# Other durations for small matmuls and for GpSimd's DMA issues in the planner of a fused attention and two-layer kernel

## The chip, the cores and the metric

One core of a Trainium2 chip runs the whole program. The metric is the device time of one execution in microseconds (us), the median of several runs. The core has five engines, each with its own instruction queue worked off in order: TensorE (PE), VectorE (DVE), ScalarE (ACT), GpSimd (POOL) and SyncE (SP). A DMA is issued from one of these queues, here from SP's and POOL's, and the queue stands still while its next instruction waits for a semaphore.

## The reference

```python
gamma = 1.0 - 2.0 ** (-5.0 - np.arange(H))              # B=4, H=8, S=768, D=64
for t in range(S):
    state = gamma * state + einsum('bhd,bhe->bhde', k[:, :, t], v[:, :, t])
    y[:, :, t] = scale * einsum('bhd,bhde->bhe', q[:, :, t], state)
x = y as 3072 tokens x 512
h = x @ w_in;   x = (h * sigmoid(1.702 h)) @ w_out      # 512 -> 2048 -> 512
h = x @ w2_in;  g = P(h) / Q(h);  out = g @ w2_out      # rational function, 512 -> 2048 -> 512
```

Everything is fp32. The kernel keeps that accuracy by splitting each operand of the two layers into a high and a low part and running three products of them.

## The kernel before

The program has three stretches. Up to some 138 us a first block of work is emitted in an order written out by hand (the steps 0 to 13 of layer 1 with the attention chunks they need). From about 138 to 608 us runs the rest of layer 1, interleaved with attention and with the preparation of layer 2's weights; this is the stretch that a list scheduler orders. From 608 us to the end layer 2 runs by a planner of its own.

In the middle stretch the code calls the engines as usual, but while `nc.on` is set each call is only recorded, as an operation of the class `Deck`. `Deck.cost` (L281) gives it a duration from its engine and its shape. `Deck.plan` (L314) then plays the program: it always takes the engine that can go on earliest and of its ready operations the one that was recorded first; a DMA's landing is estimated from its size and its run length. `Deck.flush` (L370) emits the operations in the planned order, so that each engine's queue follows the plan. All instructions of this stretch therefore carry L375 in the profile; L390 is work that was not recorded. Calls inside `with nc.group(extra)` stay together as one operation whose duration is their sum plus `extra`. The order within each engine is fixed by this plan; at run time only semaphores decide when an instruction starts. Tiles of one pool tag share slots, and the plan decides which slot a tile gets and which earlier reader it must wait for.

Attention runs in 24 chunks of 128 tokens, six for each batch. Chunks 8 to 23 belong to the recorded stretch. The names of a chunk c, which the later sections use with the chunk's number behind them:

- q and k are loaded "turned" by 16 small DMAs each (`load_turned`), q's on SyncE's queue, k's on GpSimd's, into slots of the tag "raw". These slots appear in the profile under the name of whoever opened them (`turnq_slot`, `turnk_slot`, `rawk_slot`, `rawv_slot`): the turned q of chunk 18, for example, lies in `turnk_slot`.
- `att_turn` multiplies the turned q with a table on VectorE (`<-turnq_slot,qtab`) and transposes both (`STREAM_TRANSPOSE qT`, `kT`). A transpose ends the use of its raw slot.
- `y_unit(c)` (L1533) issues a group of small 64x64 matmuls on TensorE: the sums of the state and the outputs of the chunk's first half. It needs the masked scores sm(c) (two VectorE products, `sm_slot<-pS_slot,cs`). VectorE then makes the two states st (`st_slot<-pS_slot,st_slot`). The unit ends with the load of turned q and k of chunk c + 2.
- `z_unit(c)` (L1544) issues the outputs of the second half, which need the states, and the scores of chunk c + 1, which need qT and kT of c + 1. The masks sm(c + 1) follow on VectorE. `out` and `lows` copies turn the outputs into high and low parts (`xh`, `xl`).

y16, z16 and so on below are the groups of small matmuls of these units. Between two such groups TensorE runs the large matmuls (128x512 output) of layer 1: `hp_slot<-xh_slot,wi` for the hidden layer, `o_slot<-gh_slot,wo` for its output, with `gl` and `gh` the parts of the activation, made on VectorE and ScalarE.

Beside that, `conv2` prepares layer 2's weights: a 512 KB load on SyncE into a staging tile (`os`, `sumb`, `a`), a first pass on ScalarE into `u`, a handful of passes on VectorE (`TENSOR_SCALAR`, `SCALAR_TENSOR_TENSOR`, `TENSOR_TENSOR` on `os`, `sumb`, `a`, `u`), and a store to `wc` or `wo` in DRAM on GpSimd. A staging tile is loaded anew once its stores have been read out.

Of the kernel before, what the change touches and what calls it, by code (L numbers as in the profile page):

```python
# [233 lines left out]
class Deck:  # L234
# [46 lines left out]
    def cost(self, engine, method, out, views):  # L281
        if method == "dma_start":
            size = 1
            for v in views[:1]:
                size = v.at.size * (P // ROWS if v.home.space != "dram" else 1)
            return (0.4 if engine == "sync" else 0.7), size * 4
        n = int(np.prod(out.shape[1:])) if isinstance(out, View) else 64
        if engine == "tensor":
            return (0.2267 if n >= 512 else 0.0178 * n / 64), None
        if engine == "scalar":  # L290
            return 0.19 + n * 0.00083, None
        if method == "tensor_scalar":
            return 0.155 + n * 0.00052, None
        return 0.155 + n * 0.00104, None
# [515 lines left out]
def tile_kernel(ctx: ExitStack, tc: tile.TileContext, q, k, v, w1i, w1o, w2i, w2o, pa, pb, cst, out):  # L810
    nc = Deck(tc)
# [280 lines left out]
    def load_raw(c, nm, pool=None, tag="raw", at=None):  # L1092
        b, cc = divmod(c, NCH)
        src = {"q": q, "k": k, "v": v}[nm][b, :, cc * P : (cc + 1) * P, :]
        t = at
        if t is None:
            t = (pool or raws).tile([P, H, D], F32, tag=tag, name=f"raw{nm}{c}")
        if nm == "v" or (c < 4 and nm == "q"):
            nc.sync.dma_start(out=t, in_=src.rearrange("h t d -> t h d"), run=256)
        else:  # L1100
            pairs = t.rearrange("t (p n) d -> t n p d", n=2)
            for n in range(2):
                nc.sync.dma_start(out=pairs[:, n], in_=src[NP * n : NP * n + NP].rearrange("p t d -> t p d"), run=256)
        RAW[c, nm] = t
# [29 lines left out]
    def scale_v(c, eng):  # L1134
        v_ = RAW[c, "v"]
        f = tab["k"][:, c % NCH, :]
        if eng is nc.scalar:
            for x in range(H):
                h = v_[:, NP * (x % 2) + x // 2]
                nc.scalar.activation(out=h, in_=h, func=ACTF.Copy, scale=f[:, x : x + 1])  # L1140
        else:
            o = v_.rearrange("a (n p) d -> a n p d", n=2)
            g = f.rearrange("a (p n) -> a n p", n=2)
            eng.tensor_tensor(out=o, in0=o, in1=g.unsqueeze(3).to_broadcast([P, 2, NP, D]), op=ALU.mult)
# [5 lines left out]
    def ps(tag, nm):  # L1150
        if tag in "ah":
            return (ps_a if tag == "a" else ps_h).tile([P, NP, P], F32, tag=tag, name=nm)
        return ps_o.tile([P, NP, P], F32, tag=tag, name=nm)
# [18 lines left out]
    def load_turned(c, nm, eng):  # L1172

        b, cc = divmod(c, NCH)
        src = {"q": q, "k": k}[nm][b, :, cc * P : (cc + 1) * P, :]
        t = raws.tile([P, NP, P], F32, tag="raw", name=f"turn{nm}{c}")
        for g in range(4):
            for p in range(NP):
                eng.dma_start(
                    out=t[32 * g : 32 * g + 32, p, :].rearrange("j (b i) -> j b i", i=32),  # L1180
                    in_=src[NP * (g // 2) + p, :, 32 * (g % 2) : 32 * (g % 2) + 32].rearrange("(b j) i -> j b i", j=32),
                    run=128,
                )
        RAW[c, nm + "T"] = t
# [15 lines left out]
    def scores(c, pss, col, flip):  # L1200

        qT, kT = QK[c, "q"], QK.pop((c, "k"))
        for p in range(NP):
            for n in range(2):
                for x in range(2):
                    r, w = HALF[n], HALF[x]
                    nc.tensor.matmul(
                        pss[n ^ flip][w, col + 64 * p : col + 64 * p + 64], kT[r, p, w], qT[r, p, w],
                        start=(p == 0), stop=True, skip_group_check=True,
                    )  # L1210

    def masks(c, pss, col, flip, alt=None):
        sm = at_tile(c, "sm", alt).rearrange("a (n x) t -> a n (x t)", n=2).rearrange("a n (p t) -> a n p t", t=D)
        for n in range(2):
            nc.vector.tensor_tensor(
                out=sm[:, n], in0=pss[n ^ flip][:, col : col + 4 * D].rearrange("a (p t) -> a p t", t=D), in1=mask, op=ALU.mult
            )
        SM[c] = sm
# [47 lines left out]
    def state_sums(c, pss, begun):  # L1266

        kr, vr = RAW.pop((c, "k")), RAW[c, "v"]
        for p in range(NP):
            for x in state_halves(c):  # L1270
                for n in range(2):
                    w = HALF[x]
                    nc.tensor.matmul(
                        pss[x][HALF[n], 4 * D + 64 * p : 4 * D + 64 * p + 64], kr[w, 2 * p + n, :], vr[w, NP * n + p, :],
                        start=(x, n) not in begun, stop=True, skip_group_check=True,
                    )
                    begun.add((x, n))

    def states_of(c, pss):

        state = ST.get(c)
        for x in state_halves(c):
            pk = pss[x][:, 4 * D :].rearrange("a (p e) -> a p e", e=D)
            t = (at1, sp)[x].tile([P, NP, D], F32, tag=("mid", "st")[x], name=f"st{x}_{c}")
            if state is None:
                nc.vector.tensor_copy(out=t, in_=pk)
            else:
                nc.vector.tensor_tensor(out=t, in0=pk, in1=state, op=ALU.add)
            state = t
            ST[(c, "mid") if x == 0 else c + 1] = t  # L1290

    def att_S(c, tg, alt=None, sums=True):
        pss = [ps(tg[n], f"pS{n}_{c}").rearrange("a x t -> a (x t)") for n in range(2)]
        with nc.group(0.25):
            scores(c, pss, 0, 0)
        if sums:
            state_sums(c, pss, {(x, n) for x in range(2) for n in range(2)})
        masks(c, pss, 0, 0, alt)
        if sums:
            states_of(c, pss)  # L1300
# [222 lines left out]
    def out_home(c):  # L1523
        bi, cc = divmod(c, 4)
        if bi < NB:
            if cc == 0:
                x_tiles(bi)
            return (*X[1, bi], cc * P)
        t = at.tile([P, H, D], F32, tag="raw", name=f"so{c}")
        t = SO[c] = t.rearrange("a (n k h) d -> a n k (h d)", n=2, k=2)  # L1530
        return [t[:, 0], t[:, 1]], None, 0

    def y_unit(c):  # L1533
        with nc.group(0.25):
            att_Y0(c, ("a", "a"), *out_home(c), True, PIECES)
        PIECES[c][0]()
        states_of(c, PY[c])
        if c + 1 < NT // P:
            scale_v(c + 1, nc.vector)
        if c + 2 < NT // P:  # L1540
            load_turned(c + 2, "q", nc.sync)
            load_turned(c + 2, "k", nc.gpsimd)

    def z_unit(c):  # L1544
        py = PY.pop(c)
        _, second, outs, lows = PIECES.pop(c)
        with nc.group(0.25):
            second()
            if c + 1 < NT // P:
                scores(c + 1, py, 4 * D, 1)  # L1550
        outs()
        if c + 1 < NT // P:
            masks(c + 1, py, 4 * D, 1)
        lows()
        if c + 2 < NT // P:
            load_raw(c + 2, "k")
            load_raw(c + 2, "v")

    def s_unit(c):
        att_S(c, ("a", "a"), None, False)  # L1560
        scale_v(c, nc.vector)
        att_turn(c + 1)
# [14 lines left out]
    for c in range(FLAT, NT // P):  # L1577
        n = c - FLAT
        todo[Y_AT[n]].append(lambda c=c: y_unit(c))
        todo[Z_AT[n]].append(lambda c=c: z_unit(c))  # L1580
        if c + 2 < NT // P:
            todo[TURN_AT[n]].append(lambda c=c: att_turn(c + 2))
# [18 lines left out]
    with tc.manual_schedule(engines={E.SP}):  # L1601
# [198 lines left out]
        with tc.manual_schedule(engines={E.PE, E.DVE, E.Activation, E.Pool}):  # L1800
# [109 lines left out]
            for i in range(FIRST_STEPS, NS - 2):  # L1910
# [12 lines left out]
                layer, bi, fc, t0, n = steps[i]  # L1923
# [193 lines left out]
```

## Time and profile before

| | before |
|---|---|
| median of 3 runs | 1101.42 us (1100.48 to 1102.96) |
| profiled execution, own time | 1104.64 us |
| its span | 1102.8 us |
| granted TensorE clock, mean | 0.999 of full speed |
| TensorE busy | 1087.5 us, 99% of the span |
| VectorE busy | 872.2 us, 79% |
| ScalarE busy | 698.5 us, 63% |
| GpSimd busy | 208.0 us, 19% |

The profile is of one execution, whose own time lies 3.22 us above the median; of its time 1.84 us lie outside the span. A timeline row gives the start of an instruction (or of several alike in a row) from the span's start, its length, engine, line, operation with output and inputs, count, and in brackets the idle time just before it with what ended it. The instructions of one engine overlap a little, so the distance of two starts is a better measure of a cost than the length.

### The profile page before, as it was taken

To read this page: it belongs to the slowest core of one execution; us is meant where nothing else is said; L and a number is where in the kernel's file an instruction comes from. 1 tells how busy PE (TensorE), PEld (TensorE's weight loads), DVE (VectorE), ACT (ScalarE), POOL (GpSimd) and SP (SyncE) were. 2 spreads that over 40 slices of the span, in tenths; PEclk is the share of its full clock that TensorE was granted. 3 is DMA by queue.
4 is the path that set the end of the run, shared out by engine and by line. 5 is a ranking of instruction groups with operands and counts; after the bars stand their busy time and mean duration, and the time that the engine had idled before them with its cause. 6 is when DMAs were issued, how large, how long until landed. Compare 5 with 4: busy or idle time off the path is not lost.

```text
span 1102.8 us, 19408 instructions
## 1 busy us (share of the span) xinstructions
PE 1087.5 (99%) x7169; PEld 883.0 (80%) x7169; DVE 872.2 (79%) x1262; ACT 698.5 (63%) x1105; POOL 208.0 (19%) x368
## 2 busy tenths in 40 slices
PE   8999999999999999999999999999999999999998
PEld 6678878888877778888888888888888888888886
DVE  6898556356745679789995799998988897899895
ACT  5898422233323346667763788787787886787882
POOL 0003346545675601133102000000000000000000
PEclk9999999999999999999999999999999999999999
DMA  9964336546776775798878775832454913454011
GB/s 229 318 174 131 77 113 165 141 103 153 194 195 158 219 233 200 236 364 311 290 254 329 267 247 202 315 153 86 126 153 130 333 51 96 124 162 117 19 39 39
DMA packets 192703, 199.76 MB, mean 181 GB/s; under 512 B 108512, under 2 KB 140768, under 8 KB 192608
## 3 DMA queue, kind: packets, MB, share of 16 engines
q1 hardware_dynamic: 172960, 154.45, 46.7%
q0 software_dynamic: 19648, 44.06, 11.5%
q8 instruction: 57, 0.93, 0.4%
q14 instruction: 38, 0.31, 0.1%
HBM read 139.73 MB, written 58.72 MB: 180 GB/s over the span
## 4 chain that ended last, share of the span: by engine, by line
PE 78%; POOL 5%; DMA 5%; SPq 5%; issue 3%; DVE 1%; ACT 1%; DVEq 0%; POOLq 0%; ACTq 0%
PE o L390 26%; PE o_slot L375 14%; PE hp_slot L375 13%; PE a L390 12%; PE c L390 6%; SPq L390 3%; PE b L390 3%; PE hp L390 3%; POOL turnk_slot L375 2%; SPq L375 2%; POOL rawk_slot L375 2%; POOL rawv_slot L375 2%; PE pS_slot L375 1%; DMA os_slot<-in_moe_w_in_dram 1%; DMA s<-in_moe_w_out_dram 1%
## 5 line engine op out<-in xcount | busy, mean ns | idle before, releaser
L375 PE MATMUL o_slot<-gh_slot,wo 128*128 128x512 f32 x480 | 161.7, 393 | 0.0
L375 PEld LDWEIGHTS o_slot<-gh_slot,wo 128*128 128x128 f32 x480 | 90.1, 188 | 19.3
L375 ACT ACTIVATE z_slot<-hp_slot 128x512 f32<-128x512 f32 x56 | 33.4, 596 | 107.8 <-PE hp_slot L375 107.8
L390 PE MATMUL a<-x,wi 128*128 128x512 f32 x384 | 97.5, 389 | 0.0
L375 PE MATMUL o_slot<-gl_slot,wo 128*128 128x512 f32 x240 | 93.5, 390 | 0.0
L375 POOL DMA_DIRECT2D turnk_slot<-in_k_dram x144 | 80.3, 559 | 60.7 <-DVE kT_slot L375 38.7
L375 PE MATMUL hp_slot<-xh_slot,wi 128*128 128x512 f32 x256 | 85.3, 394 | 0.0
L375 PE MATMUL hp_slot<-xl_slot,split_slot 128*128 128x512 f32 x336 | 84.7, 389 | 0.0
L390 PEld LDWEIGHTS a<-x,wi 128*128 128x128 f32 x384 | 72.1, 188 | 15.0
L390 DVE SCALAR_TENSOR_TENSOR z<-z,ab,w 128x1024 f32<-128x1024 f32 x48 | 61.5, 1280 | 28.4 <-ACT w L390 28.4
L375 PEld LDWEIGHTS hp_slot<-xl_slot,split_slot 128*128 128x128 f32 x336 | 63.1, 188 | 13.1
L390 ACT ACTIVATE gh<-h 128x1024 fp32r<-128x1024 f32 x48 | 50.9, 1060 | 34.1 <-PE o L390 33.6
L390 DVE SCALAR_TENSOR_TENSOR gl<-h,gh 128x1024 fp32r<-128x1024 f32 x48 | 58.5, 1219 | 5.4 <-ACT gh L390 5.4
L390 ACT ACTIVATE w<-z,ab 128x1024 f32<-128x1024 f32 x48 | 55.1, 1152 | 12.1 <-DVE z L390 12.1
L390 DVE TENSOR_TENSOR p<-h,p 128x1024 f32<-128x1024 f32 x48 | 58.5, 1219 | 4.4 <-ACT p L390 4.4
L390 DVE SCALAR_TENSOR_TENSOR p<-p,ab,h 128x1024 f32<-128x1024 f32 x48 | 61.4, 1280 | 0.3
L390 DVE SCALAR_TENSOR_TENSOR p<-p,ab,w 128x1024 f32<-128x1024 f32 x48 | 61.3, 1279 | 0.0
L390 ACT ACTIVATE p<-h,ab 128x1024 f32<-128x1024 f32 x48 | 59.6, 1241 | 0.0
L390 DVE SCALAR_TENSOR_TENSOR z<-z,w 128x1024 f32<-128x1024 f32 x48 | 58.5, 1219 | 1.1 <-ACT w L390 0.9
L390 PE MATMUL o<-wo_slot,gh 128*128 128x512 f32 x192 | 59.1, 389 | 0.0
L390 ACT ACTIVATE z<-h 128x1024 f32<-128x1024 f32 x48 | 50.7, 1061 | 12.6 <-DVE h L390 12.1
L390 DVE SCALAR_TENSOR_TENSOR h<-z,p 128x1024 f32<-128x1024 f32 x48 | 58.4, 1219 | 0.2
(369 smaller groups left out, 2745.2 us busy)
## 6 DMA issues: line engine op xcount, KB each, us to landing
wi<-wc SPq DMA_DIRECT2D x168, 256.0 KB, 2.8
x<-xc SPq DMA_DIRECT2D x28, 512.0 KB, 8.4
s<-in_moe_w_in_dram SPq DMA_DIRECT2D x16, 512.0 KB, 7.8
s<-in_moe_w_out_dram SPq DMA_DIRECT2D x16, 512.0 KB, 6.8
ring_slot<-wd SPq DMA_DIRECT2D x56, 128.0 KB, 4.1
wc<-os_slot POOLq DMA_DIRECT2D x11, 512.0 KB, 4.8
xc<-xo SPq DMA_DIRECT2D x10, 512.0 KB, 4.5
out_dram<-os SPq DMA_DIRECT2D x10, 512.0 KB, 3.0
```

The lines of the kernel that those rows point to most:

```text
L375: fn(*[self.real(x) for x in args], **{k: self.real(x) for k, x in kw.items()})
L390: return fn(*[d.real(x) for x in args], **{k: d.real(x) for k, x in kw.items()})
```

## The change

Four numbers of the planner's costs: a DMA issue on GpSimd's queue counts 0.57 us instead of 0.7; a matmul of fewer than 512 columns counts 0.0295 us for each 64 columns instead of 0.0178; and the three groups of small matmuls in `att_S`, `y_unit` and `z_unit` get 0.24 us on top instead of 0.25. No instruction is added, removed or altered. Since the plan is made from these numbers, the order of every engine's queue in the middle stretch is made anew, and with it which tile lies in which slot.

```diff
--- before.py
+++ after.py
@@ -283,10 +283,10 @@
             size = 1
             for v in views[:1]:
                 size = v.at.size * (P // ROWS if v.home.space != "dram" else 1)
-            return (0.4 if engine == "sync" else 0.7), size * 4
+            return (0.4 if engine == "sync" else 0.57), size * 4
         n = int(np.prod(out.shape[1:])) if isinstance(out, View) else 64
         if engine == "tensor":
-            return (0.2267 if n >= 512 else 0.0178 * n / 64), None
+            return (0.2267 if n >= 512 else 0.0295 * n / 64), None
         if engine == "scalar":
             return 0.19 + n * 0.00083, None
         if method == "tensor_scalar":
@@ -1291,7 +1291,7 @@
 
     def att_S(c, tg, alt=None, sums=True):
         pss = [ps(tg[n], f"pS{n}_{c}").rearrange("a x t -> a (x t)") for n in range(2)]
-        with nc.group(0.25):
+        with nc.group(0.24):
             scores(c, pss, 0, 0)
         if sums:
             state_sums(c, pss, {(x, n) for x in range(2) for n in range(2)})
@@ -1531,7 +1531,7 @@
         return [t[:, 0], t[:, 1]], None, 0
 
     def y_unit(c):
-        with nc.group(0.25):
+        with nc.group(0.24):
             att_Y0(c, ("a", "a"), *out_home(c), True, PIECES)
         PIECES[c][0]()
         states_of(c, PY[c])
@@ -1544,7 +1544,7 @@
     def z_unit(c):
         py = PY.pop(c)
         _, second, outs, lows = PIECES.pop(c)
-        with nc.group(0.25):
+        with nc.group(0.24):
             second()
             if c + 1 < NT // P:
                 scores(c + 1, py, 4 * D, 1)
```

The first place is around chunk 17's turned q. On SyncE's queue, the difference (- before, + changed); `turnq_slot<-in_q x16` are the loads of q17, `os_2_slot<-in_moe_w_out` a staging load for the conversion of weights:

```order
 L375 DMA rawv_slot<-in_v_dram 128x8x64
-L375 DMA turnq_slot<-in_q_dram 32x4x32 x16
-L375 DMA rawk_slot<-in_k_dram 128x4x64 x2
 L375 DMA os_2_slot<-in_moe_w_out_dram 128x1024
+L375 DMA turnq_slot<-in_q_dram 32x4x32 x16
+L375 DMA rawk_slot<-in_k_dram 128x4x64 x2
 L375 DMA sumb_slot<-in_moe_w_in_dram 128x4x256
 L375 DMA a_slot<-in_moe_w_in_dram 128x4x256
 L375 DMA rawv_slot<-in_v_dram 128x8x64
```

The staging load has moved ahead of the 16 loads of q17 and the two of `rawk`.

On VectorE at the same place, before (`sm_slot` are both masks of chunk 16, `turnq_slot,qtab` is the product of q17, `xl` the low parts of an output):

```order
L375 TENSOR_TENSOR sm_slot<-pS_8_slot,cs 128x256 x2
L375 TENSOR_TENSOR xl_0_slot<-pS_8_slot,xh_0_slot 128x2x64 x2
L375 TENSOR_TENSOR xl_1_slot<-pS_8_slot,xh_1_slot 128x2x64 x2
L375 TENSOR_TENSOR turnq_slot<-turnq_slot,qtab 128x512
L375 STREAM_TRANSPOSE qT_slot<-turnq_slot 128x512
L375 TENSOR_SCALAR os_2_slot<-os_2_slot 128x512
```

And in the changed kernel:

```order
L375 TENSOR_TENSOR os_2_slot<-u_slot,os_2_slot 128x512
L375 TENSOR_TENSOR turnq_slot<-turnq_slot,qtab 128x512
L375 TENSOR_TENSOR sm_slot<-pS_8_slot,cs 128x256 x2
L375 TENSOR_TENSOR xl_0_slot<-pS_8_slot,xh_0_slot 128x2x64 x2
L375 TENSOR_TENSOR xl_1_slot<-pS_8_slot,xh_1_slot 128x2x64 x2
L375 STREAM_TRANSPOSE qT_slot<-turnq_slot 128x512
L375 TENSOR_SCALAR sumb_slot<-sumb_slot 128x512
```

The product of q17 has moved from behind the masks of chunk 16 to ahead of them.

The second place is VectorE from the transpose kT17 to the masks of chunk 17, before (`st_9` is the second state of chunk 16; `u`, `os`, `a`, `sumb` belong to the conversion; the two `sm` are chunk 17's; the product of q18 comes seven rows below the last one):

```order
L375 STREAM_TRANSPOSE kT_slot<-turnk_slot 128x512
L375 TENSOR_TENSOR st_9_slot<-pS_8_slot,st_8_slot 128x256
L375 TENSOR_SCALAR u_slot<-u_slot 128x512
L375 SCALAR_TENSOR_TENSOR u_slot<-u_slot,a_slot 128x512
L375 TENSOR_TENSOR os_0_slot<-u_slot,os_0_slot 128x512
L375 SCALAR_TENSOR_TENSOR u_slot<-a_slot,u_slot 128x512
L375 TENSOR_TENSOR os_2_slot<-u_slot 128x256
L375 TENSOR_SCALAR u_slot<-u_slot 128x512
L375 SCALAR_TENSOR_TENSOR u_slot<-u_slot,sumb_slot 128x512
L375 TENSOR_TENSOR sm_slot<-pS_8_slot,cs 128x256
L375 TENSOR_TENSOR gl_slot<-z_slot,gh_slot 128x512
L375 TENSOR_TENSOR sm_slot<-pS_8_slot,cs 128x256
```

In the changed kernel, from kT17 on:

```order
L375 STREAM_TRANSPOSE kT_slot<-turnk_slot 128x512
L375 TENSOR_SCALAR u_slot<-u_slot 128x512
L375 SCALAR_TENSOR_TENSOR u_slot<-u_slot,a_slot 128x512
L375 TENSOR_TENSOR os_0_slot<-u_slot,os_0_slot 128x512
L375 TENSOR_TENSOR rawv_slot<-rawv_slot,cs 128x512
L375 SCALAR_TENSOR_TENSOR u_slot<-a_slot,u_slot 128x512
L375 TENSOR_SCALAR u_slot<-u_slot 128x512
L375 SCALAR_TENSOR_TENSOR u_slot<-u_slot,sumb_slot 128x512
L375 TENSOR_TENSOR gl_slot<-z_slot,gh_slot 128x512
L375 TENSOR_TENSOR st_8_slot<-pS_8_slot,st_8_slot 128x256
L375 TENSOR_TENSOR st_9_slot<-pS_8_slot,st_8_slot 128x256
```

The second state now stands ten instructions behind kT17 instead of directly behind it. Seven rows further down, still in the changed kernel, with `turnk_slot,qtab` the product of q18:

```order
L375 TENSOR_TENSOR a_slot<-os_2_slot,a_slot 128x2x256
L375 TENSOR_TENSOR turnk_slot<-turnk_slot,qtab 128x512
L375 TENSOR_TENSOR sm_slot<-pS_8_slot,cs 128x256
L375 TENSOR_TENSOR gl_slot<-z_slot,gh_slot 128x512
L375 TENSOR_TENSOR sm_slot<-pS_8_slot,cs 128x256
L375 STREAM_TRANSPOSE qT_slot<-turnk_slot 128x512
```

Both masks of chunk 17 have moved from ahead of the product of q18 to behind it.

The third place is TensorE at z21, the difference (the three rows with `pS` are z21's, the second half's outputs and the scores of chunk 22):

```order
 L375 MATMUL hp_slot<-xl_1_slot,wi_5_802 128x512
 L375 MATMUL hp_slot<-xh_1_slot,wi_5_802 128x512
+L375 MATMUL pS_8_slot<-qT_slot,st_8_slot 64x64 x8
+L375 MATMUL pS_8_slot<-sm_slot,rawk_slot 64x64 x8
+L375 MATMUL pS_8_slot<-qT_slot,kT_slot 64x64 x16
 L375 MATMUL o_0_slot<-gh_slot,wo_3_slot 128x512
 L375 MATMUL o_0_slot<-gl_slot,wo_3_slot 128x512
```

The group has moved ahead of nine large matmuls `o_slot<-gh_slot,gl_slot,wo_3`, behind which it stood before. On the rest of TensorE's queue only four pieces of output further on change places with products of layer 2's input; on GpSimd's queue some stores to `wd`, `wc` and `wo` change places with the loads of k11, k12, k18, k19 and k20.

## Rows read from the trace of the kernel before

**Rows 1.** Waits of TensorE from 138 to 620 us: releaser, total, times, longest
```profile
PE pS_slot L375 <- DVE kT_slot L375: 3.8, 3, 2.5
...
PE pS_slot L375 <- ACT rawk_slot L375: 0.5, 1, 0.5
PE pS_slot L375 <- ACT turnq_slot L375: 0.4, 1, 0.4
PE pS_slot L375 <- DVE st_slot L375: 0.2, 1, 0.2
```

**Rows 2.** Timeline of TensorE: start, length, line, operation, count [idle before, releaser]
```profile
150.09 0.95 PE L375 MATMUL pS_slot<-rawv,rawk 64*64 64x64 f32 x30 [1.82 <-DVE sm_slot L375]
150.84 0.22 PE L375 MATMUL pS_slot<-qT,st 64*64 64x64 f32 x2
...
290.96 0.69 PE L375 MATMUL pS_slot<-rawv_slot,rawk_slot 64*64 64x64 f32 x32
291.47 0.41 PE L375 MATMUL pS_slot<-qT_slot,st_slot 64*64 64x64 f32 x16
...
297.72 0.46 PE L375 MATMUL pS_slot<-qT_slot,st_slot 64*64 64x64 f32 x16
...
304.48 0.62 PE L375 MATMUL pS_slot<-rawv_slot,rawk_slot 64*64 64x64 f32 x14
...
330.86 0.69 PE L375 MATMUL pS_slot<-qT_slot,kT_slot 64*64 64x64 f32 x32 [2.50 <-DVE kT_slot L375]
...
376.32 0.39 PE L375 MATMUL o_slot<-gl_slot,wo_slot 128*128 128x512 f32 x1
376.55 0.39 PE L375 MATMUL o_slot<-gh_slot,wo_slot 128*128 128x512 f32 x1
...
378.78 0.69 PE L375 MATMUL pS_slot<-qT_slot,kT_slot 64*64 64x64 f32 x32 [1.08 <-DVE kT_slot L375]
```

**Rows 3.** Timeline of VectorE, 282 to 329 us
```profile
282.69 0.76 DVE L375 TENSOR_TENSOR sm_slot<-pS_slot,cs 128x256 f32<-128x256 f32 x2 [1.69 <-PE pS_slot L375]
...
287.07 0.69 DVE L375 TENSOR_TENSOR turnq_slot<-turnq_slot,qtab 128x512 f32<-128x512 f32 x1 [2.40 <-DMA rawk_slot<-in_k_dram]
...
296.25 0.70 DVE L375 STREAM_TRANSPOSE kT_slot<-turnk_slot 128x512 f32<-128x512 f32 x1
...
297.18 0.41 DVE L375 TENSOR_SCALAR u_slot<-u_slot 128x512 f32<-128x512 f32 x1
...
302.09 0.43 DVE L375 TENSOR_TENSOR sm_slot<-pS_slot,cs 128x256 f32<-128x256 f32 x1
...
308.78 0.69 DVE L375 TENSOR_TENSOR turnk_slot<-turnk_slot,qtab 128x512 f32<-128x512 f32 x1 [3.33 <-DMA turnk_slot<-in_q_dram]
...
328.40 0.43 DVE L375 TENSOR_SCALAR os_slot<-os_slot 128x512 int32<-128x512 uint32 x1 [2.31 <-DMA os_slot<-in_moe_w_out_dram]
```

**Rows 4.** Timeline of SyncE's DMA issues, 273 to 306 us
```profile
273.95 9.66 SPq L375 DMA_DIRECT2D turnq_slot<-in_q_dram  x16
...
285.38 0.45 SPq L375 DMA_DIRECT2D os_slot<-in_moe_w_out_dram  x1
...
286.47 0.39 SPq L375 DMA_DIRECT2D a_slot<-in_moe_w_in_dram  x1
...
296.98 8.47 SPq L375 DMA_DIRECT2D turnk_slot<-in_q_dram  x16
```

**Rows 5.** Timeline of GpSimd's DMA issues, 264 to 277 us
```profile
264.79 8.62 POOL L375 DMA_DIRECT2D turnk_slot<-in_k_dram  x15 [10.05 <-DVE kT_slot L375]
...
275.95 0.72 POOL L375 DMA_DIRECT2D wc<-os_slot  x1 [0.74 <-DVE os_slot L375]
```

**Rows 6.** DMA issues at 284 and 276 us: count, KB each, us to landing
```profile
os_slot<-in_moe_w_out_dram SPq DMA_DIRECT2D x1, 512.0 KB, 4.5
...
a_slot<-in_moe_w_in_dram SPq DMA_DIRECT2D x1, 512.0 KB, 7.2
...
wc<-os_slot POOLq DMA_DIRECT2D x1, 512.0 KB, 3.6
```

## The prediction

> **What bounds the kernel now.** I read the page's busy shares first: TensorE is busy nearly all of the span, so a gain can only come out of its few waits, and a loss is any new one. Next the waits of TensorE in the list-scheduled stretch [rows 1, 2]: 3.8 us for kT in three waits, 0.5, 0.4 and 0.2 for copies and a state, and 1.82 for masks, 6.8 us in all. Then TensorE's rows around its groups of small matmuls [rows 2], for the place of each wait and the length of a group. Last what VectorE, SyncE and GpSimd do ahead of those groups [rows 3 to 6].
>
> Two things are to be seen there. First, the 1.82 us at 150.09 lie in front of the first recorded unit and wait for masks made before any of the new order takes effect; so at most 6.8 - 1.8 = 5.0 us can be won. Second, the kernel's groups stand where their inputs are ready only just: z16 started at 297.72 [rows 2], while the last mask of chunk 17, which y17 needs at 304.48, was made at 302.09 [rows 2, 3]. The order of VectorE has about 2 us of slack here, and the new order spends more.
>
> **The figures themselves.** A group of 32 small matmuls takes 291.47 - 290.96 = 0.51 us, 16 ns for each [rows 2]. The old figure is 17.8 ns, the new one 29.5 ns. A y or z unit has 64: the old plan gives it 64 x 0.0178 + 0.25 = 1.39 us, the new one 64 x 0.0295 + 0.24 = 2.13 us. By the row it is 64 x 0.016 = 1.04 us and a few tenths around it. So each of some 30 units becomes 0.74 us too long in the plan, and over the stretch the plan's TensorE falls behind the real one by 30 x 0.74 = 22 us. Work that TensorE waits for is then planned later among the other engines' work than it is needed. The GpSimd figure goes the other way: 15 issues in 8.62 us are 0.575 us each [rows 5], so 0.57 is right and 0.7 was too long.
>
> A row that speaks against this reading is the first unit's: 30 small matmuls in 150.84 - 150.09 = 0.75 us, 25 ns each [rows 2]. It is the group just behind a wait; the groups that come without one run at 16 ns, so I take 16. The Trainium skill, FP8 and Floating Point Precision, section TensorE Precision Notes, says that true FP32 makes four passes through the array, and TensorEngine Tiling (Array Packing), section Key Properties, that 64x64 tiles run independently; an estimate from these pages at the full clock is 64 x 4 columns / 2.4 GHz / 4 tiles = 27 ns, beside which the new figure would be the truer one and the sum would be rival 1's 1096.4 us; the 16 ns of the trace do not agree.
>
> **What moves, and what it costs.** No instruction is added or taken away; I follow the new order by hand through the durations of the rows.
>
> *SyncE ahead of q of chunk 17.* The load os_2<-w_out now stands ahead of the 16 loads of turned q17, behind it before. It overwrites a staging tile whose content a GpSimd store must first have read. That store was issued at 275.95 and took 3.6 us to land [rows 5, 6], so unmoved it would be done at 279.55. It stands behind the 16 turned loads of k16, which wait for the transpose kT15; that transpose now stands four VectorE instructions earlier. Nine VectorE instructions between 297.18 and 302.09 take 4.91 us [rows 3], 0.546 each, so k16's loads start 2.2 us earlier than 264.79 [rows 5] and the store is done at 277.35. With 0.45 us for the issue itself, as at 285.38, q17's loads start at 277.8 instead of 273.95 [rows 4]: 3.85 later (bounds 0.5, if the store is long done, to 6.1).
>
> *Masks of chunk 16.* On VectorE both masks sm16 now stand behind q17's product with its table, ahead of it before. The product ran at 287.07 [rows 3] and goes to 290.95; 0.69 for it and 0.76 for the masks (their row at 282.69) end at 292.4, and TensorE starts y16 then instead of at 290.96 [rows 2]: +1.4 (0 to 3.7).
>
> *kT17 and the state of chunk 16.* SyncE's load of a for the weights' conversion was issued at 286.47 [rows 4]. One issue before it is gone (0.45 and a small gap, 0.5) and all is 3.85 later: 289.8. It landed after 7.2 us; the nearest load of the same size took 4.5 [rows 6]. I take 7.2, the same tile: 297.0 (294.3 at the shortest). kT17 stands behind VectorE's pass over a and one more product now, 3 x 0.546 = 1.6 with its own: it ends at 298.6 (295.9), where it ended at 296.25 + 0.70 = 296.95 [rows 3]. The Trainium skill, DMA: Bandwidth & Descriptors, section Anatomy of one DMA — SWDGE (gpsimd) path, fits 2.0 us plus bytes / 436e3, for 512 KB an estimate of 3.2 us; beside it the whole sum would come out some 4 us smaller, but the rows' 4.5 and 7.2 do not agree with it.
>
> Behind kT17 ten VectorE instructions, mostly conversion, come before the second state st1 of chunk 16 is done, which z16 needs; in before it was the next one. 10 x 0.546 = 5.5 us: st1 and z16 at 304.1 instead of 297.72 [rows 2], 6.4, of which 1.4 is y16's: +5.0 more.
>
> *Masks of chunk 17.* Both sm17 now stand behind q18's product, which stood seven instructions behind them. q18's loads take the slot that kT17 frees: they began at 296.98, just as kT17 ended, and the product came at 308.78 [rows 3, 4], 11.8 us later. From 298.6 this is 310.4; four instructions (it, a mask, a product, a mask) at 0.546 end at 312.6, where y17 starts instead of at 304.48: +8.1 in all (z16 at 304.1 plus the 304.48 - 297.72 = 6.76 us between the two would give 310.9, so the last 1.7 are this wait's). At the short landing it is 309.9, +5.4.
>
> *Later.* z18's 2.50 us at 330.86 came from kT19 behind a pass over os that waited 2.31 us for its load at 328.40 [rows 2, 3]. A pass over another weight load stands ahead of kT19 again, but TensorE comes 8 us later and that load only some 5 to 8: between nothing and 2.5 is left; I take 1.0, a gain of 1.5. z21 moves ahead of nine large matmuls on TensorE. Its second half waited 1.08 us for kT22 at 378.78 [rows 2], so whatever is moved behind it adds to this wait; a large matmul starts 376.55 - 376.32 = 0.23 us after another [rows 2], nine are 2.1, of which I keep 2.0: +2.0 (0 to 2.6). States of chunks 19, 20 and 22 stand behind one to six conversion instructions: 0 to 0.546 x 6 = 3.3, I take 0.5, as most of these waits overlap. Later sum +1.0 (-2.5 to +5.9). After 394 us no group of small matmuls is left; four swaps of output pieces with products of the second layer follow where TensorE waited for nothing: 0, hidden by the full queue of either kind (0 to 0.5 if one input is late).
>
> **The sum.** 1.4 + 5.0 + 1.7 + 1.0 = +9.1 us. The profiled execution took 1104.64 us, 3.22 above the median of 1101.42; it would become 1113.7, and the median 1110.5.
>
> **Rivals.** *1, faster.* The truer issue figure on GpSimd puts k's loads, transposes and states in time, and every wait but the first unit's vanishes: 1101.42 - 5.0 = 1096.4. For it speak the 0.575 us and the first unit's 25 ns, against it that sm16 and sm17 now stand behind loads that were not needed for them. It decides if q17's and q18's products come no later than 289.5 and 302.3. *2, same.* The store is long done, the a load lands in 4.5: a issued at 286.4, there at 290.9, kT17 done at 292.6, q18's product at 304.4, y17 at 306.6, +2.1, and z18's 2.5 us take it back: 1101. *3, slower, but less.* The store's delay is as computed, the landing short: +5.4 at y17, given back in part at z18 and z21 (-2.5 to 0): 1104.3 to 1106.8. *4, slower still.* The a load and q18 slip by the store's full bound (2.2 more), and the later terms reach their upper half (+3): 1115.7.
>
> **How the numbers follow.** Forecast 0.46, rival 1 0.10, rival 2 0.12, rival 3 0.24, rival 4 0.08. A measurement of this kernel can tell about 0.2%, 2.2 us, from no change. Faster 0.10, same 0.12, slower 0.78. The range, 1101.5 to 1115.5, leaves out rival 1, half of rival 2 and the end of rival 4.
>
> **What would show it.** TensorE rows: a wait for sm at y16 (about 1.5 us), one for st at z16 (about 5), one for sm at y17 (1 to 3), and z21's wait near 3. On SyncE the row of os_2<-w_out ahead of q17's loads, with q17's first issue near 278; on VectorE q18's product near 310 with sm17 behind it. It is wrong if q17's loads still start at 274 and kT17 ends before 293, or if the waits sum to less than 6.8 us.

## The result, and the profile after

The changed kernel took 1115.03 us (median of 4 runs, 1113.82 to 1116.52), the kernel before beside it 1102.19 (1100.48 to 1103.83): a ratio of 1.0117, 95% interval 1.0096 to 1.0138. The forecast was 1110.5. By these medians the change costs 12.8 us. The profiled execution took 1115.13 us, 10.5 more than before's 1104.64.

Page of the changed kernel: span, busy time of the engines, and the granted TensorE clock in 40 slices.

```profile
span 1113.4 us, 19396 instructions
...
PE 1091.6 (98%) x7169; PEld 886.8 (80%) x7169; DVE 872.5 (78%) x1262; ACT 698.0 (63%) x1105; POOL 207.0 (19%) x368
...
PEclk9999999999999899999999999999999999999999
```

VectorE, ScalarE and GpSimd were busy as long as before, within 1 us. TensorE issued the same 7169 matmuls, but was busy for 4.1 us more than before's 1087.5, and one slice of its clock has dropped. Its waits from 138 to 640 us (releaser, total, times, longest), beside which [rows 1] stand for before:

```profile
PE pS_slot L375 <- ACT rawv_slot L375: 4.3, 1, 4.3
PE pS_slot L375 <- DVE st_slot L375: 4.2, 2, 4.0
PE pS_slot L375 <- DVE xl_slot L375: 2.5, 1, 2.5
PE o_slot L375 <- DVE os_slot L375: 1.2, 1, 1.2
PE pS_slot L375 <- DVE sm_slot L375: 0.6, 1, 0.6
```

They sum to 12.8 us, against 6.7 before: the 4.9 of [rows 1] and the first unit's 1.8 of [rows 2] (the single waits, unrounded, give the prediction's 6.8). So the span's 10.6 us more are 6.1 of waits, 4.1 of busy time and 0.4 elsewhere. The waits by place, in the timeline of TensorE (start, length, line, operation, count, idle before and its releaser):

```profile
291.84 0.82 PE L375 MATMUL pS_slot<-rawv_slot,rawk_slot 64*64 64x64 f32 x30 [2.47 <-DVE xl_slot L375]
...
302.86 1.05 PE L375 MATMUL pS_slot<-qT_slot,st_slot 64*64 64x64 f32 x14 [4.00 <-DVE st_slot L375]
...
304.19 1.10 PE L375 MATMUL pS_slot<-qT_slot,kT_slot 64*64 64x64 f32 x30
...
312.06 0.62 PE L375 MATMUL pS_slot<-rawv_slot,rawk_slot 64*64 64x64 f32 x14
...
383.83 0.48 PE L375 MATMUL pS_slot<-qT_slot,st_slot 64*64 64x64 f32 x4 [4.27 <-ACT rawv_slot L375]
384.47 0.59 PE L375 MATMUL pS_slot<-qT_slot,st_slot 64*64 64x64 f32 x10 [0.15 <-DVE st_slot L375]
...
385.18 0.37 PE L375 MATMUL pS_slot<-qT_slot,kT_slot 64*64 64x64 f32 x2
...
385.34 1.10 PE L375 MATMUL pS_slot<-qT_slot,kT_slot 64*64 64x64 f32 x30
...
386.96 0.63 PE L375 MATMUL o_slot<-gl_slot,wo_slot 128*128 128x512 f32 x1
387.39 1.05 PE L375 MATMUL o_slot<-gh_slot,wo_slot 128*128 128x512 f32 x2
...
396.29 0.69 PE L375 MATMUL pS_slot<-rawv_slot,rawk_slot 64*64 64x64 f32 x32
```

The rows with waits are y16, z16 and z21; 312.06 is y17, 396.29 is y22. Two waits of the list are not shown as rows: 0.6 us at the first recorded unit, where before waits 1.82 [rows 2], and 1.2 us at 360.28 for VectorE's copy of an output (`os_slot<-o_slot`), where before waits for nothing. y17 has no wait and is late all the same: from z16 to y17 it is 312.06 - 302.86 = 9.20 us, where the same work took 304.48 - 297.72 = 6.76 in [rows 2]. The rows between show why: 30 small matmuls take 1.10 us (32 took 0.69 in [rows 2]), and behind z21 a large matmul starts 387.39 - 386.96 = 0.43 us after another instead of 0.23. Busy time and granted clock of TensorE in 5-us stretches of the changed kernel (stretch, its length, busy (count), clock, share of the DMA engines, GB/s):

```profile
295.00:300.00 5.00, 3.86 (x18) 1.00 0.13 24
300.00:305.00 5.00, 2.14 (x64) 0.59 0.57 156
305.00:310.00 5.00, 5.00 (x26) 0.72 0.53 132
310.00:315.00 5.00, 5.00 (x66) 1.00 0.97 300
...
380.00:385.00 5.00, 1.01 (x24) 0.78 0.66 158
385.00:390.00 5.00, 5.00 (x61) 0.53 0.50 162
390.00:395.00 5.00, 5.00 (x23) 1.00 0.31 62
```

Before, the clock is 1.00 in all of these stretches. In the changed kernel it falls to its 1.2 GHz level in the 4-us waits ahead of z16 and z21 and is back at 2.4 GHz some 5 us later; the shares in the table are the mean over the two levels. Each fall costs a little over 2 us: 9.20 - 6.76 = 2.4 behind z16. Behind z21, from the first matmul with kT22 (385.18) to y22 it is 11.11 us; before it was 385.75 - 378.78 = 6.97 ([rows 2] and the row of y22 below) and the nine large matmuls that z21 moved past add 9 x 0.23 = 2.07, so 2.1 remain; the slow first half of z21 (383.83 to 385.18) is not counted in this. The term is not in the prediction.

```profile
385.75 0.69 PE L375 MATMUL pS_slot<-rawv_slot,rawk_slot 64*64 64x64 f32 x32
```

VectorE of the changed kernel, where the inputs of these groups are made:

```profile
289.40 0.69 DVE L375 TENSOR_TENSOR turnq_slot<-turnq_slot,qtab 128x512 f32<-128x512 f32 x1 [4.30 <-DMA rawk_slot<-in_k_dram]
290.01 0.75 DVE L375 TENSOR_TENSOR sm_slot<-pS_slot,cs 128x256 f32<-128x256 f32 x2
291.10 0.88 DVE L375 TENSOR_TENSOR xl_slot<-pS_slot,xh_slot 128x128 fp32r<-128x128 f32 x4 [0.34 <-ACT xh_slot L375]
...
296.32 0.43 DVE L375 TENSOR_SCALAR a_slot<-a_slot 128x512 int32<-128x512 uint32 x1 [1.08 <-DMA a_slot<-in_moe_w_in_dram]
...
297.26 0.70 DVE L375 STREAM_TRANSPOSE kT_slot<-turnk_slot 128x512 f32<-128x512 f32 x1
...
302.39 0.88 DVE L375 TENSOR_TENSOR st_slot<-pS_slot,st_slot 128x256 f32<-128x256 f32 x2
...
309.15 0.69 DVE L375 TENSOR_TENSOR turnk_slot<-turnk_slot,qtab 128x512 f32<-128x512 f32 x1 [2.62 <-DMA turnk_slot<-in_q_dram]
...
310.85 0.42 DVE L375 TENSOR_TENSOR sm_slot<-pS_slot,cs 128x256 f32<-128x256 f32 x1
...
378.69 0.69 DVE L375 TENSOR_TENSOR rawv_slot<-rawv_slot,qtab 128x512 f32<-128x512 f32 x1 [6.75 <-DMA xq_slot<-x]
...
383.06 0.42 DVE L375 TENSOR_TENSOR st_slot<-pS_slot,st_slot 128x256 f32<-128x256 f32 x1
```

The order is to be read from the top: the masks of chunk 16 (290.01) stand behind the product of q17, which waited for its loads; kT17 and the states st16 (302.39) stand behind the pass over `a`, which waited for its load; st21 (383.06) stands behind the product of q22, which waited 6.75 us, and six conversion passes. On ScalarE the last step towards z21, a copy, waits in turn for st21:

```profile
383.51 0.27 ACT L375 COPY rawv_slot<-pS_slot 128x128 f32<-128x128 f32 x1 [2.72 <-DVE st_slot L375]
```

SyncE's issues in the changed kernel, beside [rows 4]:

```profile
275.13 0.35 SPq L375 DMA_DIRECT2D os_slot<-in_moe_w_out_dram  x1
275.60 10.61 SPq L375 DMA_DIRECT2D turnq_slot<-in_q_dram  x16
...
288.40 0.46 SPq L375 DMA_DIRECT2D a_slot<-in_moe_w_in_dram  x1
...
297.99 8.87 SPq L375 DMA_DIRECT2D turnk_slot<-in_q_dram  x16
```

### The profile page after: what moved, and what is told of

The parts are those of the page before. It is cut to its first block, busy times and chain, and to the rows that moved or that the text cites. A ratio compares the mean times of both kernels' runs of the same rounds, so it can differ in the third digit from the quotient of the medians.

```text
span 1113.4 us, 19396 instructions
## 1 busy us (share of the span) xinstructions
PE 1091.6 (98%) x7169; PEld 886.8 (80%) x7169; DVE 872.5 (78%) x1262; ACT 698.0 (63%) x1105; POOL 207.0 (19%) x368
## 4 chain that ended last, share of the span: by engine, by line
PE 83%; DMA 3%; issue 3%; SPq 3%; POOL 3%; DVE 2%; ACT 1%; DVEq 0%; POOLq 0%; ACTq 0%
PE o L390 26%; PE o_slot L375 17%; PE hp_slot L375 14%; PE a L390 12%; PE c L390 6%; PE b L390 3%; PE pS_slot L375 3%; PE hp L390 3%; SPq L390 2%; POOL turnk_slot L375 1%; DMA s<-in_moe_w_out_dram 1%; SPq L375 1%; POOL turnq_slot L375 1%; DMA a_slot<-in_moe_w_in_dram 1%; DVE os_slot L375 0%
```

## The experiments

The ratios are against the kernel before run beside them, whose medians were 1105.22 us (e1 to e4), 1104.38 (e5 to e8), 1103.23 (e9 to e11) and 1103.89 (e12); they can differ from the quotient of the two medians by 0.001. The changed kernel was not run beside them; its 1.0117 was measured separately. A profile shows one execution of its kernel. Eight kernels put single recorded operations at other places of one engine's row after the plan. `MOVES` lists the engine, the operations, those behind which they are put, and an offset in rows; names carry the chunk, with q for the product with the table, c for ScalarE's copy, l for loads, w0o for the store of one piece of w_out. The cuts show the lines that matter; the function `moved`, which does the moving, and the naming of operations are left out.

**Undoing one place.** e1 puts st16 back directly behind kT17.

```diff
-        order = self.plan()
+        order = self.moved(self.plan())
+    MOVES = [('vector', ('st16',), ('kT17',))]
```

> The changed kernel, but both states of chunk 16 follow kT17 on VectorE directly, as before the change, instead of standing ten instructions behind it. Theory A (waits take each other's place): z16 waits under 1 us instead of 4.0, TensorE's clock stays up behind it, but y17 then waits about 1.7 us for the masks of chunk 17, which still stand behind q18's product at about 309, and by z19 at most 0.8 us of the gain is left. Time 0 to 0.8 us below the changed kernel's, ratio to the kernel before 1.011. Theory B (the terms add up): the wait of 4.0 and the 2.4 us of slow matmuls behind it are both gained: 6 us, ratio 1.006.

Measured: 1115.0 us, 1.0089 (1.0074 to 1.0104). TensorE's row of z16:

```profile
300.38 0.71 PE L405 MATMUL pS_slot<-qT_slot,st_slot 64*64 64x64 f32 x16 [3.37 <-ACT turnq_slot L405]
```

The states are ready at 296.7 and z16 waits on, now for a copy on ScalarE that stands behind an activation over `sumb`, itself waiting for a VectorE pass. One late input was removed, and the next one lets z16 start 2.5 us earlier than in the changed kernel's profile; the table of one order below shows that z16 starts as early in another execution without this edit.

e2 puts the products of q17 and q18 back behind the low parts of chunk 15 and the masks of chunk 17.

```diff
+    MOVES = [('vector', ('q17',), ('xl15',)), ('vector', ('q18',), ('sm17',))]
```

> The changed kernel, but q17's product stands behind the masks of chunk 16 and the low parts of chunk 15, and q18's product behind the masks of chunk 17, as before the change. Theory A: y16 no longer waits (2.47 us before), but z16 starts at about 302.9 all the same, since its state stands behind kT17 and that behind a load, so its wait grows to about 6 us; y17 waits for nothing, as now. Time 0 to 0.7 us below the changed kernel's, ratio 1.011. Theory B: 2.5 us at y16 and 0.8 at y17 are gained, ratio 1.009.

Measured: 1113.84 us, 1.0071 (1.0054 to 1.0088). y16 has no wait, and z16 waits longer:

```profile
302.00 1.04 PE L405 MATMUL pS_slot<-qT_slot,st_slot 64*64 64x64 f32 x14 [5.91 <-DVE st_slot L405]
```

It starts 0.86 us earlier than in the changed kernel. So y16's term and z16's do not add: z16 is set by VectorE's row, whenever y16 ran. That the edit is what removed y16's wait is not shown: in e1, which leaves q17's product where the change put it, y16 does not wait either.

e3 moves the product and transpose of q22 behind st21, and leaves st21 behind its conversion passes.

```diff
+    MOVES = [('vector', ('q22', 'qT22'), ('st21',))]
```

> The changed kernel, but q22's product and transpose stand behind the states of chunk 21 on VectorE, and so behind nothing that z21 needs but kT22. Both theories: the first part of z21 waits for nothing (4.27 us now), its second part for kT22 about 1 to 2 us, and TensorE's clock stays up behind it (granted 0.53 there now, 2.3 us). Time 4.5 to 5.5 us below the changed kernel's, ratio 1.007. If the clock's fall is not caused by the wait, only 2.3 to 3.3 us are gained, ratio 1.009.

Measured: 1116.24 us, 1.0094 (1.0068 to 1.0121); z21 still waits 5.31 us for ScalarE. The conversion passes ahead of st21 now wait for their own input: the first stands at 379.35 behind 6.14 us of idle VectorE, for an activation on ScalarE that waited for a weight load until 378.66. st21 ends at 383.77 in e3 and at 384.42 in the changed kernel. What both theories expected, no wait at the first part of z21, did not come.

e4 makes these three edits together.

```diff
+    MOVES = [('vector', ('q17',), ('xl15',)), ('vector', ('st16',), ('kT17',)), ('vector', ('q18',), ('sm17',)), ('vector', ('q22', 'qT22'), ('st21',))]
```

> The three edits of the other runs together. Theory A: y16 waits for nothing, z16 about 2.5 us (kT17 stands behind a load), y17 for nothing, z17 or z18 2 to 3 us for their transposes, which follow loads that began no earlier; the gain at z21 is kept. 5.5 to 7.5 us below the changed kernel's, ratio 1.006. Theory B: all new waits and slow stretches are gone, 2.5 + 4.0 + 2.4 + 5 = 14 us, ratio 0.999.

Measured: 1117.71 us, 1.0102 (1.0079 to 1.0126); z16 waits 5.23 us and z21 5.59, both for ScalarE. The theory that each place can be given back by its own edit, and that the gains add, falls.

**Clearing one place on every queue.** e5 clears z16 on VectorE, ScalarE and GpSimd: the states, the masks and kT17 ahead of the conversion, the copy five rows earlier, and the store that delays SyncE behind the loads of k18.

```diff
+    MOVES = [('vector', ('q17',), ('xl15',), 0), ('vector', ('kT17',), ('qT17',), 0), ('vector', ('gl40',), ('kT17',), 0), ('vector', ('st16',), ('gl40',), 0), ('vector', ('sm17',), ('st16',), 7), ('vector', ('gl41',), ('sm17',), -1), ('scalar', ('c16',), (), -5), ('gpsimd', ('w0o',), ('k18l',), 0)]
```

> The changed kernel, but around chunks 16 to 18 the attention steps stand ahead of the weights' conversion on three queues at once: on VectorE q17's product behind the masks of chunk 16, kT17, a gl and the states of chunk 16 directly behind qT17, the masks of chunk 17 ahead of q18's product; on ScalarE the copy that frees z16's PSUM bank ahead of the conversion's passes; on GpSimd k18's loads ahead of a weight store. Theory C (the conversion's work at the head of several queues holds z16): y16, z16 and y17 wait less than 1 us each, the clock stays up, q18's loads start near 293.5 instead of 298.0, and everything up to z19 comes 5 to 7 us earlier; the waits at z21 stay. Ratio to the kernel before 1.002 to 1.005. Rival D (the transfers are late and no order helps): z16 still waits 3 us or more, ratio 1.008 to 1.010.

Measured: 1115.66 us, 1.0103 (1.0067 to 1.0138). z16's wait is gone; y17 waits 1.79 us, and z17 waits nearly as long as z16 did, for st17 behind the next group of conversion passes:

```profile
315.10 0.70 PE L402 MATMUL pS_slot<-qT_slot,st_slot 64*64 64x64 f32 x16 [3.57 <-DVE st_slot L402]
```

e6 does the same for z21: st21 directly behind its masks, the work of chunk 22 behind it.

```diff
+    MOVES = [('vector', ('st21',), ('sm21',), 0), ('vector', ('q22', 'qT22', 'kT22'), ('st21',), 0)]
```

> The changed kernel, but on VectorE the states of chunk 21 stand directly behind its masks, and q22's product, qT22 and kT22 ahead of the six conversion instructions that stood ahead of z21's inputs. Theory C: z21 waits 1 to 2 us instead of 4 to 5, and the clock stays up behind it: 3 to 5 us below the changed kernel's, ratio 1.005 to 1.007. Rival D (q22's load itself is late): z21 still waits 3 us or more, ratio 1.008 to 1.010.

Measured: 1113.31 us, 1.0078 (1.0052 to 1.0104). z21 waits 1.75 us, but z22 took its place:

```profile
398.24 0.85 PE L402 MATMUL pS_slot<-qT_slot,st_slot 64*64 64x64 f32 x14 [3.50 <-DVE st_slot L402]
```

e7 is e5 and e6 in one.

```diff
+    MOVES = [... e5's eight ..., ... e6's two ...]
```

> The edits of the last two runs together. Theory C: the gains add, 8 to 11 us below the changed kernel's, ratio 0.999 to 1.003; what is left are waits of 1 to 3 us at z18 and z21, as the kernel before has them. Rival D: ratio 1.008 or more.

Measured: 1114.91 us, 1.0090 (1.0065 to 1.0115); neither z16 nor z21 waits over 1.3 us, and y17, z17 and z22 wait 2.28, 3.55 and 2.94. The gains do not add.

e6 shows one thing more. The traces of e3 and e6 have the changed kernel's order on all five queues up to VectorE's row at 378.69, and e1's has it up to the row at 297.89. Up to there they are further executions of one order, and the waits differ all the same (us):

| | y16 waits | load of `a`, from issue to landing | z16 waits |
|---|---|---|---|
| changed kernel | 2.47 | 7.8 | 4.00 |
| e3 | 0.24 | 8.3 | 5.83 |
| e6 | 1.91 | 5.5 | none |
| e1 | none | 8.1 | (its states are moved) |

z16 in e3, then the pass over `a` and z16 in e6, where the clock also fell behind y16 (0.81 from 295 to 300), so that TensorE came to z16 later:

```profile
303.65 1.04 PE L405 MATMUL pS_slot<-qT_slot,st_slot 64*64 64x64 f32 x14 [5.83 <-DVE st_slot L405]
...
293.55 0.43 DVE L402 TENSOR_SCALAR a_slot<-a_slot 128x512 int32<-128x512 uint32 x1 [0.47 <-DMA a_slot<-in_moe_w_in_dram]
...
300.54 0.46 PE L402 MATMUL pS_slot<-qT_slot,st_slot 64*64 64x64 f32 x16
```

So the waits of y16 and z16 are not a fixed price of the order; the landing of the load of `a` has a share in z16's, and e1, e2 and e5 cannot show by one profile each that their edits took them away. z21's wait is steadier: 4.27 us in the changed kernel, and 3.64, 4.62 and 4.65 in e1, e2 and e5, which leave its place on VectorE alone. The times, medians of several executions, stand.

**The figures one by one.** e8 keeps 0.57 and takes the small matmul from the trace: 16.3 ns, with nothing on top of the three groups (the second pair of lines stands in three places).

```diff
-            return (0.2267 if n >= 512 else 0.0295 * n / 64), None
+            return (0.2267 if n >= 512 else 0.0163 * n / 64), None
-        with nc.group(0.24):
+        with nc.group(0.0):
```

> The kernel before with the planner's figures as the trace has them: 0.0163 us for a small matmul, nothing on top of a group, 0.57 us for an issue on GpSimd. Theory F (the nearer the figures to the trace, the fewer waits): below the kernel before by up to 5 us, ratio 0.996 to 1.000. Rival G (the plan's other errors, above all the landing times of loads, decide, and any new order is a draw): a wait of 2 us or more at some other chunk, ratio 1.000 to 1.008.

Measured: 1103.0 us, 0.9998 (0.9973 to 1.0024). All of the loss is gone. TensorE's waits in e8:

```profile
PE pS_slot L375 <- DVE kT_slot L375: 4.0, 2, 3.3
PE pS_slot L375 <- ACT rawv_slot L375: 1.3, 1, 1.3
PE hp_slot L375 <- DVE split_slot L375: 0.4, 1, 0.4
```

5.7 us, and its busy time is 1087.4 us, before's. There is still one wait of 3.35 us (z17, for kT18 behind a pass over `a`), as rival G expected, while the time fits theory F: the run does not part the two. Part of the smaller sum is the first unit's wait: here its masks run at 141.64 on VectorE, while in the kernel before they run at 149.62, behind a pass that waited for a store, and the 1.82 us of [rows 2] are gone.

e9 has the new small-matmul figure alone, e10 the new GpSimd figure alone.

```diff
-            return (0.4 if engine == "sync" else 0.57), size * 4
+            return (0.4 if engine == "sync" else 0.7), size * 4
-        with nc.group(0.24):
+        with nc.group(0.25):
```

> The kernel before with only the small matmuls' figure changed, 0.0295. Theory H (the figure that lies further from the trace does the harm: the plan's TensorE falls behind, and conversion work is put ahead of attention steps): most of the loss is there, ratio to the kernel before 1.006 to 1.011, with waits at z16 and z21 and the clock falling behind the longest. Theory J (any new order is a draw of its own, and the loss belongs to the two figures together): ratio 0.998 to 1.004.

```diff
-            return (0.2267 if n >= 512 else 0.0295 * n / 64), None
+            return (0.2267 if n >= 512 else 0.0178 * n / 64), None
-        with nc.group(0.24):
+        with nc.group(0.25):
```

> The kernel before with only the figure of GpSimd's issues changed, 0.57, which is nearer to the trace's 0.575. Theory H: no loss, 0.997 to 1.003, waits as in the kernel before but at other chunks. Theory J: likewise within 0.998 to 1.004, so this run tells them apart only together with the other one; a ratio over 1.006 speaks against H.

Measured: e9 1112.79 us, 1.0093 (1.0062 to 1.0124); e10 1109.9 us, 1.0058 (1.0038 to 1.0079). In both, z21 carries most of it. TensorE in e9:

```profile
381.10 1.04 PE L375 MATMUL pS_slot<-qT_slot,st_slot 64*64 64x64 f32 x14 [6.23 <-DVE st_slot L375]
```

and 6.45 us in e10, each with a slow clock behind it; y16 and z16 do not wait in either profile. The second state of chunk 16 stands five (e9) and three (e10) instructions behind kT17 there, not ten, so that order at z16 needs both figures; for y16 this is not shown, since e10 too has q17's product ahead of the masks of chunk 16. The table by the plan's duration of a unit of 64 small matmuls, with the extra:

| issue on GpSimd | 1.04 us (e8) | 1.39 us | 2.13 us |
|---|---|---|---|
| 0.7 us | not run | 1 (before) | 1.0093 (e9) |
| 0.57 us | 0.9998 (e8) | 1.0058 (e10) | 1.0117 (the change) |

Along each row the time rises with a unit that is planned too long, as the prediction's reading of the figures says; with five cells, a draw of good and bad orders that happens to fall in this sequence is not excluded. At 1.39 us the truer issue figure alone costs 0.6%, which that reading did not say; at 2.13 the intervals of the two ratios overlap.

e11 is e8 with kT18 and kT22 put directly behind qT18 and qT22, where e8's two remaining waits come from.

```diff
+    MOVES = [('vector', ('kT18',), ('qT18',), 0), ('vector', ('kT22',), ('qT22',), 0)]
```

> The plan with the trace's figures (0.0163, 0 and 0.57), and kT18 and kT22 each directly behind qT18 and qT22 on VectorE. In that plan z17 waited 3.35 us for kT18, which stood behind a pass that waited 5.9 us for the load of its weights. If such passes ahead of the attention steps set the time, z17 waits for nothing, q19's loads begin near 304.5 instead of 312.0 and all later steps come earlier: 3 to 4 us, ratio to the kernel before 0.996 to 0.998. If another step takes the wait over, ratio 0.999 to 1.002.

Measured: 1102.44 us, 0.9981 (0.9964 to 0.9997): below the kernel before by little, and not told apart from e8. z17's wait is gone; q19's loads begin at 310.21, 1.8 us earlier than in e8 (312.04) instead of 7.5, and y19, z19 and z21 wait 0.91, 1.52 and 2.23 us.

**A common cause?** Passes that wait for weight loads stand ahead of the attention steps on VectorE or ScalarE at z16 and z21, and at z17 in e8. e12 keeps the changed figures and lets the planner land DMAs of long rows later.

```diff
-                op.end = moving + 1.6
+                op.end = moving + (1.6 if run < 1024 else 4.5)
```

> The changed kernel's figures are kept; the planner's landing of a DMA of long rows (the 512 KB weight loads and stores and v) is put 2.9 us later (4.5 instead of 1.6 us behind its transfer). In the new order one conversion pass stands between the transpose qT22 and the state st21 instead of six, and seven instructions between kT17 and st16 instead of nine. Theory L, the loss comes from weight loads that the plan lands too early, so that passes over them head the queues: z16 and z21 wait under 2 us each, the granted clock stays at 1.00 around both, ratio to before at most 1.004 (1104 to 1107 us). Theory W, waits take each other's place whatever single cause is removed: z21's wait falls to 1 to 2 us, z16's stays at 3 to 5 us with a lower clock behind it, or a new wait of over 2 us comes in a chunk that had none; ratio 1.006 to 1.011 (1109 to 1115 us).

Measured: 1112.64 us, 1.0077 (1.0064 to 1.0091). Its profile has none of the waits of y16, z16 and z21, at a clock of 1.00, yet only about a third of the loss is won back. TensorE's largest waits now, with the row of VectorE ahead of each:

```profile
148.51 0.69 DVE L375 TENSOR_TENSOR turnq_slot<-turnq_slot,qtab 128x512 f32<-128x512 f32 x1 [6.23 <-DMA turnq_slot<-in_q_dram]
...
149.59 0.48 PE L375 MATMUL pS_slot<-rawv,rawk 64*64 64x64 f32 x4 [2.54 <-DVE sm_slot L375]
...
574.34 0.68 DVE L375 COPY sumb_slot<-o_slot 128x512 f32<-128x512 f32 x1
...
575.08 0.50 PE L375 MATMUL o_slot<-gh_slot,wo_slot 128*128 128x512 f32 x1 [1.78 <-DVE sumb_slot L375]
```

Both are followed by a slower clock (0.50 from 150 to 155, 0.66 from 575 to 580), and TensorE's busy time is 1093.6 us, the longest of all. At the first one before waits 1.82 us too [rows 2], and with the order that before and the changed kernel share there the wait was 0.64 us in the changed kernel and between none and 1.48 in e1 to e7; new in e12 are q's product ahead of the masks and the slow clock, and whether that clock comes from the order is open. The second stands 200 us behind z21. So an order that is planned with the later landing has none of those three waits in its profile, but it has others, and the theory of one root falls as an account of the time.

## Why the prediction was right

The direction and the places were right, and the time lies inside the range, 0.5 us below its upper end. Step by step:

- **q17's loads.** The staging load does go first and its store does hold it, but less: q17 began at 275.60, not 277.8 (273.95 in [rows 4]). The store had been issued at 268.21, 7.7 us earlier than in [rows 5] rather than the 2.2 that I worked out, and took 6.9 us to land instead of 3.6. The loads then took 10.61 us instead of 9.66.
- **y16, +1.4.** It started at 291.84 against 292.4 forecast, behind a wait of 2.47: TensorE came to it 1.6 us earlier than before, of which 1.2 are the first unit's shorter wait, which the prediction took as fixed. Its masks were done at 290.76; the last input was the low parts behind them, which I had not counted. That the product of q17 is the cause is read from the rows; e2 does not prove it, since y16 waits for nothing in e1 and 0.24 us in e3 with the product where the change put it. That the term is taken up by z16's is borne out by e2 and e3, with waits of 5.91 and 5.83 there.
- **z16, +5.0.** Right in mechanism, and in time for this profile: kT17 ended at 297.96 (298.6 forecast), z16 started at 302.86 (304.1). The load of `a` landed in 7.8 us where I took 7.2 of [rows 6]. That it came so near is in part luck: with the same order z16 waited 5.83 us in e3 and not at all in e6, where `a` landed in 5.5. The 3.2 us that the prediction sets beside this load is a fit for GpSimd's path, as the name of its section says; `a` is loaded from SyncE's queue. e1 adds what the step missed: behind st16, a copy on ScalarE holds z16 too.
- **y17, +1.7.** The time was right (312.06 against 312.6), the reason wrong. The masks of chunk 17 were done at 311.27, in time; what made y17 late is the clock, 2.4 us that no term held.
- **Later, +1.0.** This is the term that was mis-sized. z18's wait of 2.50 us vanished whole (I left 1.0), and so did z19's two, the 0.5 and 0.2 for a copy and a state in [rows 1], and 0.2 and 0.4 at z17 and z22. Against that z21 waited 4.42 us instead of 1.08, for st21 and a copy rather than for kT22 as I had it, and paid 2.1 us of slow clock behind it, and the copy at 360.28 added 1.2.
- **The sum.** +9.1 was meant as waits alone. The waits grew by 6.1 and the busy time by 4.1, so the sum came near the truth (10.5 between the profiled executions) with two errors that offset each other: 3 us of waits too many, and no term for the clock. By the medians, which differ by 12.8, the forecast was 4.5 us short; of these 3.2 are the distance of before's profiled execution from its median, which the changed kernel's (1115.13 against 1115.03) does not have.

Of the rivals, rival 4's time (1115.7) came closest, but not by its mechanism: q17's loads slipped less than I forecast, not more. Rival 1's point of decision was half met, q17's product at 289.40, while q18's came at 309.15, far behind 302.3. Its premise, that the truer GpSimd figure alone puts the steps in time, is refuted by e10. On the doubt between 16 and 25 ns for a small matmul, e8 fits 16 as the planner's figure; a plan with 25 was not run.

The Trainium skill, TensorE: Matmul & The Clock Gate, section HAM oscillation — how this bites in real kernels, says that a gap of waiting between runs of matmuls lets the gate throttle again, so that the next run starts cold. Here the trace agrees, inside a stretch where TensorE is otherwise busy 98% of the time: 0.59 and 0.72 around z16, 0.78 and 0.53 around z21.

What stays open: how much of the 12.8 us is y16's and z16's in the mean of many executions, why the truer issue figure alone costs 0.6%, and whether an order without any wait exists; in no profile here was the sum below 5.4 us.

## What to carry to other kernels

In a statically ordered kernel with one full engine, count waits of the full engine and its busy time apart: the change cost 6.1 us in the one and 4.1 in the other, and only the first can be read from an order. Even that is rough: one order had z16 waiting 4.00, 5.83 and 0 us in three executions, so what an edit does to a wait needs more than one profile of either kernel. A single late step, undone by hand, gives back a part at most when the queues behind it are just as late; seven such edits here brought the ratio from 1.0117 to between 1.0071 and 1.0103, while the planner's figure taken from the trace took away the whole loss. A truer cost figure is no gain by itself: 0.57 us is nearer to the trace than 0.7 and was slower with the old figure of the small matmul.

## What the runs showed of the hardware

A wait of a few us inside a full stretch can cost more than itself: TensorE's clock fell in the waits of 4.00 and 4.27 us, and the matmuls behind them ran at half speed until some 5 us later, 2.4 and 2.1 us lost. It did not fall in before's wait of 2.50 us nor in the changed kernel's of 2.47, but it did behind waits of 1.78 us in e12 and 1.64 in e10 (0.66 in the stretch behind each), so the length of one wait alone does not tell. The loads of 512 KB into `sumb` and `a` took 7.1 and 7.8 us to land in the changed kernel and 4.6 and 5.5 in e6, with the same order ahead of them, and a store of that size 6.9 where another in [rows 6] took 3.6.
